# A fused Fourier-mixing and SwiGLU kernel: all units split, value banks seeded from ScalarE, transforms moved to output banks

## The chip, the cores and the metric

The kernel runs on one core of a Trainium2 chip. The metric is the device time of one launch in microseconds. Before the change the median of three runs was 651.96 us (651.83 to 652.64).

## The reference

The input is mixed by the real part of a two-dimensional Fourier transform and then goes, row by row, through a gated feed-forward block:

```python
X = np.fft.fft(np.fft.fft(x, axis=1), axis=2).real      # x: 8 x 3008 x 256
g = X @ w_gate                                          # 24064 x 256 @ 256 x 1536
out = (g / (1 + np.exp(-g)) * (X @ w_val)) @ w_out      # 24064 x 1536 @ 1536 x 256
```

## The kernel before

Half of the sequence rows follow from the other half, because the transform of real data is symmetric. The kernel keeps two factors for each column of a tile (Pt and Qt, up to 512 columns). A *bank* is one buffer of the accumulation memory that matmuls write, 512 float32 columns wide; the kernel allots three to gates (g), three to values (v) and two to outputs (o). A gate or value of the "plus" row is Wp·P + Wq·Q, and that of its mirror, the "minus" row, is Wp·P − Wq·Q, except for a row d = 0 of the weights that enters both with the same sign. A *unit* is one block of 128 of the 1536 hidden columns in one tile: 12 units a tile, 24 tiles.

In an unsplit unit TensorE writes the plus value and then adds Wm·Q (Wm is −2 Wq with the d = 0 row zeroed) to get the minus value: six matmuls with the gate's three. In a *split* unit VectorE takes the half sum `es` out of the v bank before Wq·Q is added, and later forms the minus value as 2·es − v. That saves a matmul and costs VectorE an operation. `bc` is the d = 0 row of Q, broadcast to all partitions. `sv` is one of two buffers that collect the minus values and their SiLUs of a pair of units, which GpSimd multiplies into `hm`; `hp` is VectorE's product for the plus rows. The extracts here and below are shortened: index ranges are left out, and `...` marks other cuts.

```python
psG = tile_pool("psG", bufs=3, PSUM)   # g banks
psV = tile_pool("psV", bufs=3, PSUM)   # v banks
psO = tile_pool("psO", bufs=2, PSUM)   # output banks
...
SPLIT = (0, 1, 2, 3, 5, 6, 7, 8, 9, 11)                  # of 12 units, tiles 3 to 20
SPLIT_END = (0, 1, 2, 3, 4, 6, 7, 8, 9, 10, 11)          # tiles 21 to 23

def part_a(u):                         # TensorE: g, g, v (and v again where unsplit)
    ...
    if split(u):
        v = psV.tile(...)
        mm(v, Wp, 1, Pt, True, False)
        nc.scalar.activation(sg, g, AF.Silu)
        nc.vector.scalar_tensor_tensor(es, bc[t], w0[:, f], v, op0=mult, op1=add)
    ...
def part_b(u):                         # one unit later
    nc.tensor.matmul(g, Wm[:, 0, fs], Qt, start=False)
    if kept:                           # split
        nc.tensor.matmul(v, Wq[:, 1, fs], Qt, start=False)
        vm, sm = sv[:, 0, second], sv[:, 1, second]      # sv: [P, 2, 2, T]
        nc.vector.scalar_tensor_tensor(vm[:, ::-1], es, 2.0, v, op0=mult, op1=subtract)
        nc.scalar.activation(sm[:, ::-1], g, AF.Silu)
        # every second unit: GpSimd multiplies the pair into hm
        nc.vector.tensor_tensor(hp, sp, v, op=mult)
```

Between these parts each unit gives TensorE eight output matmuls of the tile before. A pair of output blocks fills a bank in 24 of them, so ScalarE copies a bank out (`ev`) in units 3, 6, 9 and 0. Fourteen *transform jobs* after the start-up (the first 50 us) produce Pt and Qt for later tiles, each in two halves; both halves were issued after one unit, in two v banks and two g banks, with `od` the copy of the first factor out of its bank. Seven of the jobs also have *one-row matmuls*, which write a single row.

## Time and profile before

| | before |
|---|---|
| median time | 651.96 us |
| span of the profiled run | 650.1 us |
| TensorE, VectorE, ScalarE, GpSimd busy | 98%, 88%, 67%, 72% |
| matmuls | 4218 |
| start-to-start gaps of TensorE, first 50 us / later | 12.2 / 8.7 us |

The last row is worked out from the starts of all matmuls: what lies between two starts beyond the first one's columns at 2.36 columns per ns, gaps of over 30 ns.

In the lines of profiles PE is TensorE, PEld its weight loads, DVE VectorE, ACT ScalarE and POOL GpSimd; L with a number is a line of the kernel. The *chain that ended last* is followed back from the last instruction, at each step to what released it.

This line of the busy time by stretches (columns: stretch, its length, then busy us and count for TensorE, its weight loads, VectorE, ScalarE and GpSimd, then clock and DMA) shows how near VectorE and GpSimd are in the middle:

```profile
200.00:300.00 100.00, 99.39 (x659) 63.17 (x658) 91.97 (x165) 67.03 (x117) 85.73 (x72) 1.00 0.41 107
```

### The profile page before, as it was taken

The numbers are of one execution on the slowest core, as the hardware profiler recorded it, in microseconds if no ns is written. First come the engines' busy times: TensorE is split into PE (matmuls) and PEld (weight loads), VectorE is DVE, ScalarE is ACT, GpSimd is POOL, SyncE is SP. The second block draws the span as 40 slices with busy tenths as digits, with TensorE's granted clock in tenths as the row PEclk, the third lists the DMA queues.
The fourth block names the chain that finished last, engine by engine and source line by source line (L and its number), as shares of the span: only waits on it lengthen the run. The fifth ranks groups of instructions, "written<-read, shape, count | busy, mean of one in ns | idle before, by whom it ended". The sixth has DMA issues, their size and how long they took to land.

```text
span 650.1 us, 12636 instructions
## 1 busy us (share of the span) xinstructions
PE 636.6 (98%) x4218; PEld 407.6 (63%) x4218; DVE 570.1 (88%) x1010; ACT 433.6 (67%) x765; POOL 467.7 (72%) x419
## 2 busy tenths in 40 slices
PE   7989999999999999999999999999999999999997
PEld 5446666666666666666666666666666666666676
DVE  8797668999998999999999989999999899899982
ACT  8576666677667676676676666766766767667663
POOL 8895955798777798897877787878787435544552
PEclk9999999999999999999999999999999999999999
DMA  9657346345215313434134112225111111111112
GB/s 225 125 75 136 107 111 167 96 135 131 76 36 110 102 44 114 125 102 109 40 107 106 48 33 67 59 75 128 50 45 37 42 42 38 45 37 46 49 50 75
DMA packets 46684, 54.36 MB, mean 84 GB/s; under 512 B 6514, under 2 KB 33690, under 8 KB 46618
## 3 DMA queue, kind: packets, MB, share of 16 engines
q1 hardware_dynamic: 43434, 51.19, 29.2%
q0 software_dynamic: 3184, 2.36, 2.6%
q8 instruction: 33, 0.54, 0.3%
q14 instruction: 33, 0.27, 0.2%
HBM read 29.39 MB, written 24.65 MB: 83 GB/s over the span
## 4 chain that ended last, share of the span: by engine, by line
PE 94%; DVE 3%; POOL 1%; ACT 1%; issue 1%; DVEq 0%; ACTq 0%; POOLq 0%
PE o L696 38%; PE g L737 19%; PE v L737 12%; PE g L767 9%; PE v L770 7%; PE v L787 2%; PE v L587 2%; PE g L587 1%; DVE Pt L600 1%; PE g L905 1%; PE g L438 1%; ACT od L595 1%; PE v L438 1%; PE v L564 1%; DVE hp L758 0%
## 5 line engine op out<-in xcount | busy, mean ns | idle before, releaser
L782 POOL TENSOR_TENSOR hm<-sv 128x1024 bf16<-128x1024 f32 (+5 forms) x126 | 249.7, 1986 | 148.1 <-DVE sv L777 138.6
L747 ACT ACTIVATE sp<-g 128x512 f32<-128x512 f32 (+2 forms) x213 | 125.4, 589 | 82.2 <-PE g L737 76.3
L696 PE MATMUL o<-Wo,hp 128*128 128x256 bf16 (+2 forms) x1140 | 169.8, 273 | 0.0
L696 PE MATMUL o<-Wo,hm 128*128 128x256 bf16 (+2 forms) x1140 | 169.7, 273 | 0.0
L749 DVE SCALAR_TENSOR_TENSOR es<-bc,w,v 128x512 f32<-128x512 bf16 (+2 forms) x213 | 155.8, 731 | 5.3 <-PE v L737 5.3
L779 ACT ACTIVATE sv<-g 128x512 f32<-128x512 f32 (+2 forms) x213 | 125.7, 590 | 45.2 <-PE g L767 44.6
L777 DVE SCALAR_TENSOR_TENSOR sv<-es,v 128x512 f32<-128x512 f32 (+2 forms) x213 | 143.9, 676 | 13.3 <-PE v L770 5.1
L696 PEld LDWEIGHTS <-hp 128*128 128x128 bf16 (+2 forms) x1140 | 112.0, 98 | 69.5
L696 PEld LDWEIGHTS <-hm 128*128 128x128 bf16 (+2 forms) x1140 | 111.9, 98 | 69.3 <-issue 0.2
L785 DVE TENSOR_TENSOR hp<-sp,v 128x512 bf16<-128x512 f32 (+2 forms) x213 | 142.6, 669 | 0.0
L737 PE MATMUL g<-Pt,Wp 128*128 128x512 bf16 (+2 forms) x288 | 108.0, 375 | 0.6
L737 PE MATMUL g<-Qt,Wq 128*128 128x512 bf16 (+2 forms) x288 | 108.0, 375 | 0.5 <-DVE Qt L600 0.5
L737 PE MATMUL v<-Pt,Wp 128*128 128x512 bf16 (+2 forms) x288 | 108.0, 375 | 0.0
L767 PE MATMUL g<-Qt,Wm 128*128 128x512 bf16 (+2 forms) x288 | 108.0, 375 | 0.0
L737 PEld LDWEIGHTS <-Wp 128*128 128x128 bf16 x576 | 56.3, 98 | 39.8 <-issue 2.5
L770 PE MATMUL v<-Qt,Wq 128*128 128x512 bf16 (+2 forms) x213 | 79.8, 375 | 0.0
L790 DVE TENSOR_TENSOR hm<-sg,v 128x512 bf16<-128x512 f32 (+2 forms) x75 | 50.8, 678 | 24.6 <-ACT sg L789 17.0
L758 DVE TENSOR_TENSOR hp<-sg,v 128x512 bf16<-128x512 f32 (+2 forms) x75 | 50.8, 678 | 14.4 <-ACT sg L757 11.3
L702 ACT COPY ev<-o 128x512 f32<-128x512 f32 x90 | 52.7, 585 | 9.8 <-PE o L696 6.1
L757 ACT ACTIVATE sg<-g 128x512 f32<-128x512 f32 (+2 forms) x75 | 44.3, 591 | 21.1 <-PE g L737 19.8
L789 ACT ACTIVATE sg<-g 128x512 f32<-128x512 f32 (+2 forms) x75 | 44.4, 593 | 17.7 <-PE g L767 17.5
L737 PEld LDWEIGHTS <-Wq 128*128 128x128 bf16 x363 | 35.5, 98 | 17.4 <-issue 2.9
(168 smaller groups left out, 595.6 us busy)
## 6 DMA issues: line engine op xcount, KB each, us to landing
out_dram<-ev SPq DMA_DIRECT2D x96, 128.0 KB
XA<-in_x_dram SPq DMA_DIRECT2D x32, 256.0 KB
XA<-in_x_dram SPq DMA_DIRECT2D x112, 64.0 KB
XC<-in_x_dram SPq DMA_DIRECT2D x32, 120.0 KB
XC<-in_x_dram SPq DMA_DIRECT2D x105, 32.0 KB
St<-Fc SPq DMA_DIRECT2D x14, 128.5 KB
out_dram<-ev SPq DMA_DIRECT2D x12, 120.0 KB
out_dram<-ev SPq DMA_DIRECT2D x10, 112.0 KB
```

Source lines behind the costliest of these rows:

```text
L696: nc.tensor.matmul(ps[:n, j, :], hts[minus][:, f, c:c + n], Wo[:, f, :], start=(f == 0), stop=(f == nF - 1))
L702: nc.scalar.copy(ev[:, 0:len(pair), :], ps[:, 0:len(pair), :])
L737: nc.tensor.matmul(ps[:, :w], Wt[:, gv, fs], src[:, :w], start=start, stop=stop, skip_group_check=True)
L747: nc.scalar.activation(sg[:, :w], g[:, :w], AF.Silu)
L749: nc.vector.scalar_tensor_tensor(es[:, :w], bc[t][:, :w], w0[:, f:f + 1], v[:, :w], op0=Alu.mult, op1=Alu.add)
L758: nc.vector.tensor_tensor(hts[t][0][:, f, :w], sg[:, :w], v[:, :w], op=Alu.mult)
L767: nc.tensor.matmul(g[:, :w], Wm[:, 0, fs], Qt[:, :w], start=False, stop=True, skip_group_check=True)
L770: nc.tensor.matmul(v[:, :wp], Wq[:, 1, fs], Qt[:, :wp], start=False, stop=True, skip_group_check=True)
L777: nc.vector.scalar_tensor_tensor(vm[:, w - 1::-1], es[:, :w], 2.0, v[:, :w], op0=Alu.mult, op1=Alu.subtract)
L779: nc.scalar.activation(sm[:, w - 1::-1], g[:, :w], AF.Silu)
L782: nc.gpsimd.tensor_tensor(hts[t][1][:, f - n + 1:f + 1, :w], sv[:, 1, 0:n, :w], sv[:, 0, 0:n, :w], op=Alu.mult)
L785: nc.vector.tensor_tensor(hts[t][0][:, f, :wp], sp[:, :wp], v[:, :wp], op=Alu.mult)
```

## The change

The intent: split all units from the fourth tile on to save TensorE 39 matmuls; pay for VectorE's extra work by giving five `es` a tile to ScalarE, which writes bc·w0 into the v bank ahead of the matmul (a *seed*) and copies the bank out after it; let the transforms use an output bank and run by halves, one unit apart. The operands of GpSimd's product are also interleaved in memory.

```diff
-        for q, pool, nm in ((0, psV, "v"), (1, psG, "g")):      # transform
+        for q, pool, nm in ((0, psO, "o"), (1, psG, "g")):
...
-    SPLIT = (0, 1, 2, 3, 5, 6, 7, 8, 9, 11)
-    SPLIT_END = (0, 1, 2, 3, 4, 6, 7, 8, 9, 10, 11)
+    SEEDED = (3, 5, 7, 9, 11)
+    SEEDED_END = (3, 5, 7, 9, 11)
     def split(u):
-        return 3 <= u[0] and u[1] in (SPLIT if u[0] < t_end else SPLIT_END)
+        return u[0] >= 3
+    def seed(u):
+        seeds[u] = psV.tile([P, T], F32, name="v")
+        nc.scalar.activation(seeds[u][:, :w], bc[t][:, :w], AF.Copy, scale=w0[:, f:f + 1])
...
-            mm(v, Wp, 1, Pt, True, False)
+            mm(v, Wp, 1, Pt, not ahead, False)
+            if ahead:
+                nc.scalar.copy(es[:, :w], v[:, :w])
+            else:
                 nc.vector.scalar_tensor_tensor(es, bc[t], w0[:, f:f + 1], v, ...)
...
-            nc.tensor.matmul(v, Wq[:, 1, fs], Qt, ...)
+            nc.tensor.matmul(v, (Wm if seeded(u) else Wq)[:, 1, fs], Qt, ...)
...
-                pending.append(svp.tile([P, 2, 2, T], F32, name="sv"))
+                pending.append(svp.tile([P, 2, T, 2], F32, name="sv"))
...
         part_a(u)
         if owork:
             owork.run(4)
+        if i + 1 < len(units) and seeded(units[i + 1]):
+            seed(units[i + 1])
...
-            whole_part(*job_at[i])
+            transform(*job_at[i])          # one half; the other after the next unit
```

Once, `Wm[:, 1]` is multiplied by −0.5, which makes it Wq without the d = 0 row.

## The prediction

> **What bounds the kernel now.** I began with the page's first part. TensorE is busy for 98% of the span, VectorE for 88%, GpSimd for 72%, ScalarE for 67%.
>
> ```profile
> PE 636.6 (98%) x4218; PEld 407.6 (63%) x4218; DVE 570.1 (88%) x1010; ACT 433.6 (67%) x765; POOL 467.7 (72%) x419
> ```
>
> The 98% alone proves little, since matmuls overlap, so I read starts in the timeline. These lines are one whole unit (one block of 128 hidden columns) in the middle of the kernel; the columns are start us, us, engine, line, operation.
>
> ```profile
> 404.84 0.38 PE L737 MATMUL g<-Pt,Wp 128*128 128x512 bf16 x1
> ...
> 405.05 0.38 PE L737 MATMUL g<-Qt,Wq 128*128 128x512 bf16 x1
> ...
> 405.27 0.38 PE L737 MATMUL v<-Pt,Wp 128*128 128x512 bf16 x1
> ...
> 405.49 0.60 PE L696 MATMUL o<-Wo,hm 128*128 128x256 bf16 x4
> ...
> 405.92 0.38 PE L767 MATMUL g<-Qt,Wm 128*128 128x512 bf16 x1
> ...
> 406.79 0.38 PE L737 MATMUL g<-Pt,Wp 128*128 128x512 bf16 x1
> ```
>
> A 512-column matmul is shown as 0.38 us but the next starts 0.216 us later; four 256-column ones take 0.43. A split unit is five of the first and eight of the second, 5 x 0.216 + 8 x 0.109 = 1.95 us, and it does take 406.79 - 404.84 = 1.95. So TensorE runs end to end here. I summed, over all starts of the trace, what each gap has beyond the matmul's own columns (at 2.36 columns per ns, the rate of these lines): 623 us of columns and 21 us of gaps. 12.2 us of the gaps lie in the first 50 us. The other 8.7 us are nearly all in the 14 transform jobs, as in this piece of the chain that ended last:
>
> ```profile
> 372.32 0.34 PE v L587 x3
> 372.66 0.02 issue
> 372.68 0.48 ACT od L595
> 373.17 0.04 issue
> 373.21 0.49 PE v L587 x3
> ```
>
> The second half of a job waits for the copy out of the first half's v bank. Seven jobs of this kind lose 0.40 us each, seven of the other kind 0.44 in two waits (for a v bank and a g bank): 5.9 us. The remaining 2.6 us are around one-row matmuls and stay.
>
> VectorE, though, is next in line. By groups with shapes apart (busy us, mean ns at the end of each line):
>
> ```profile
> L749 DVE SCALAR_TENSOR_TENSOR es<-bc,w,v 128x512 f32<-128x512 bf16 x192 | 142.6, 743 | 5.1 <-PE v L737 5.1
> L785 DVE TENSOR_TENSOR hp<-sp,v 128x512 bf16<-128x512 f32 x192 | 130.7, 681 | 0.0
> ...
> L790 DVE TENSOR_TENSOR hm<-sg,v 128x512 bf16<-128x512 f32 x60 | 41.3, 688 | 23.2 <-ACT sg L789 16.7 <-PE o L696 6.3
> ...
> L451 ACT CAST Wq<-o 128x512 bf16<-128x512 f32 x5 | 3.0, 593 | 2.2 <-PE o L447 2.2
> ...
> L453 ACT ACTIVATE Wm<-o,m 128x512 bf16<-128x512 f32 x2 | 1.4, 692 | 0.0
> ```
>
> A split unit takes three VectorE operations (0.743, 0.688, 0.681; started back to back 0.67, 0.60 and 0.60 apart, so 1.87 us against TensorE's 1.95), an unsplit one two (0.688 each). That is why not every unit was split: it saves TensorE a matmul and costs VectorE an operation.
>
> **What the Trainium skill says.** (1) "Perfetto Trace Analysis", section Identifying the Most-Contended Engine, says that matmul busy share is a poor measure, as matmuls are pipelined. The trace agrees: 0.38 us shown, 0.216 from start to start. (2) "ScalarE: Activation LUTs", section What ACT_TABLE_LOAD costs, gives about 93 ns more for each per-partition pointer operand and about 93 ns of overlap between back-to-back activations. The trace agrees: with a pointer scale 692 ns (L453) against 593 without (L451), and after a 0.585 us bank copy the next operation starts 0.48 us later. (3) "PSUM — Partial Sum Buffer", section The four PSUM rules: ScalarE's writes leave the has-written bits alone, and a matmul that opens a group clears them over its whole bank. So a seed is added to only where an earlier matmul set the bit, and a 377-column transform in a v bank would leave the later columns to be overwritten. I take this as the reason that transforms leave the v banks; no run here shows it yet. (4) "GPSIMD Engine Reference", section Performance pitfalls for Q7 kernels, puts a slow case at SBUF reads with steps above 8 bytes. The new layout steps by exactly 8, so I expect no loss; the trace of before has only unit steps here and cannot tell.
>
> **The change, part by part.**
>
> *Every unit split from the fourth tile on.* Before, 18 tiles have ten split units and three have eleven; 39 more become split. Each loses one matmul. Two units lie in a 480-column tile and one has 328, so 19720 columns go, 38.5 full matmuls x 0.217 = **8.4 us off TensorE**. That engine sets the end nearly everywhere after 50 us, so this should all reach the end unless something new waits. The instruction order confirms 39 matmuls and 39 weight loads fewer. VectorE pays 39 x (0.743 + 0.688 + 0.681 - 2 x 0.688) = 29 us more. On GpSimd, 39 single products (1.28 us) become parts of pairs (2.36 us): 39 x 1.09 = 42 us more, 468 to 510, 80%.
>
> *Seeds.* 105 units (5 in each of 21 tiles) drop the es operation on VectorE: 105 x 0.743 = 78 us less. With the 29 added, VectorE goes from 570 to 521 us. ScalarE gains a seed (a copy with pointer scale, about 0.59 + 0.10 = 0.70 us, an estimate from the two lines) and a bank copy (0.585): 105 x 1.285 = 135 us, 434 to 569, 89% by busy time. Started back to back each costs 0.1 less, so a tile of 39 operations plus transform copies holds about 20.4 us of ScalarE work in 23.6 us of TensorE work: below the bound, without much room.
>
> *What a seed can hold up.* The seed of unit u must wait for VectorE's last read of the v bank of u-3, and the matmul of u must wait for the seed. Counting from the end of the second v matmul of u-3: VectorE starts 0.2 later (as now) and finishes its two operations at about 1.55; ScalarE has done the SiLU of u-1 by then, so the seed runs from 1.62 to 2.35; TensorE reaches the seeded matmul at 0.43 + 0.65 + 0.43 + 0.43 + 0.43 + 0.43 = 2.80. So 0.45 us of slack. Only where an output copy (ev) comes just ahead of the seed does this fail: output pairs end in units 3, 6, 9 and 0, and of the seeds only that of unit 7 follows in the same slot. There the copy starts at 1.71, the seed at 2.2, and it ends at 2.9 and is seen a little later, 0.15 late. 21 tiles x 0.15 = **3 us given back**.
>
> *Transforms.* Halves one unit apart, the first factor in an output bank, which ScalarE frees within a unit. The wait for the od copy and for the v bank goes; the g bank is freed by VectorE's sums, about 1.6 us after the half, and the next half wants it 2.4 us after. I expect **5.9 us off**. An output bank is free then: pairs switch in units 3 and 6, halves come in 4 and 5.
>
> *One-off.* One scaling of a weight matrix, off the path.
>
> Sum: 652.0 - 8.4 - 5.9 + 3.0 = 640.7; I add 0.3 for unforeseen small waits: **641 us**.
>
> **Rivals.** *ScalarE becomes the next bound.* Chain: VectorE read, seed, matmul, bank copy, matmul. If ScalarE runs later than I count and every seed is late by 0.15, 105 x 0.15 = 16 us come back: 637.7 + 16 = 654, nothing gained. For it: 89% busy and strict order on one queue. Against it: today it idles mostly waiting for TensorE, as the 82.2 us ahead of its first SiLU show, and slack is 0.45 us in most slots. *GpSimd becomes the bound.* In 60 to 500 us it is busy 345 of 440 us; about 18 tiles x 2.2 us more (6 x 2.36 against 4 x 2.36 + 2 x 1.28) makes 385 of 430, 90%, and the stretch 250 to 300 us, with 43.4 of 50 now, comes near full. A pair late by more than two buffers stops VectorE and then TensorE: some 3 to 8 us, 644 to 649. If the 8-byte step also made each product half as long again, GpSimd would need about 28 us per tile and the kernel would pass 700; I hold that unlikely. If interleaving helps the two reads share lines, this rival vanishes. *Everything fits.* No late seeds: 637.7. *Transforms don't gain.* If each half finds a new wait of 0.2 us, the result is about 646.
>
> **Range and chances.** The bottom is the case where everything fits with a little gained in the start-up: 636.5. The top is GpSimd's crowding or transforms that gain nothing: 646.5. A gain of over 2% needs below about 639, more than 13 us of the 14.3 that I can find; that wants almost no late seeds: 0.25. Slower by 2% needs GpSimd's bad case: 0.03. Within 2%: 0.72.
>
> **What will show it right or wrong.** TensorE at 4179 matmuls, still 98% busy; VectorE near 521 us, ScalarE near 569, GpSimd near 510; the seed near 700 ns; the chain of waits without od between transform halves; waits of v matmuls for seeds only around unit 7, some 3 us in all. I am wrong if v matmuls wait for seeds in most units, if VectorE waits for GpSimd's products at the sv buffers, if the product of 1024 elements differs much from 2364 ns, or if the strided writes lengthen the operations that make them (0.688 on VectorE, 0.600 on ScalarE).

## The result and the profile after

The changed kernel took 645.65 us (median of 4 runs, 644.48 to 645.75), the kernel before 652.3 us in the same rounds. Ratios here are the mean time of one kernel's fast runs over that of the other's of the same rounds, so not quite the ratio of the medians: 0.9892, with a 95% interval of 0.9875 to 0.9909. The kernel is faster by 1.1%, which is within the 2% called the same.

The first part of the page of the changed kernel:

```profile
PE 632.8 (98%) x4179; PEld 405.0 (63%) x4179; DVE 522.0 (81%) x945; ACT 532.6 (83%) x975; POOL 452.3 (70%) x419
```

VectorE fell to the 521 us predicted and the 39 matmuls are gone. GpSimd went down, not up. The groups with shapes apart say why, and what the seed costs:

```profile
L794 POOL TENSOR_TENSOR hm<-sv 128x1024 bf16<-128x1024 f32 x114 | 215.9, 1894 | 130.9 <-ACT sv L791 117.1 <-DVE sv L789 12.9
L791 ACT ACTIVATE sv<-g 128x512 f32<-128x512 f32 x228 | 149.7, 656 | 6.3 <-PE g L779 6.3
...
L732 ACT ACTIVATE v<-bc,w 128x512 f32<-128x512 bf16 x95 | 67.1, 707 | 0.5 <-DVE hp L797 0.5
```

The product of a pair takes 1894 ns instead of 2364, ScalarE's SiLU that writes its operand 656 instead of 600, and the seed 707.

Next, a transform half in the chain that ended last (start us, us, what), where before stood an `od` step of 0.48 us:

```profile
371.57 0.33 PE o L587 x3
371.89 0.42 PE o L564 x3
372.31 0.43 PE g L587 x3
372.74 0.42 PE g L564 x3
373.16 0.54 PE g L743 x2
```

TensorE goes from matmul to matmul; no other engine is left in the job. What remains are the 0.09 us steps around the one-row matmuls (L564).

Two new gaps are in the timeline. The first is the one predicted, in unit 7:

```profile
398.36 0.59 ACT L698 COPY ev<-o 128x512 f32<-128x512 f32 x1
...
398.84 0.70 ACT L732 ACTIVATE v<-bc,w 128x512 f32<-128x512 bf16 x1
...
399.24 0.38 PE L743 MATMUL g<-Qt,Wq 128*128 128x512 bf16 x1
...
399.59 0.38 PE L743 MATMUL v<-Pt,Wp 128*128 128x512 bf16 x1
```

The v matmul should start 0.216 us after the g matmul, at 399.46. The seed stands behind the output copy, ends at 399.54, and the matmul starts at 399.59. The second is at a tile's start:

```profile
408.15 0.58 ACT L759 COPY es<-v 128x512 f32<-128x512 f32 x1
...
408.61 0.66 ACT L791 ACTIVATE sv<-g 128x512 f32<-128x512 f32 x1
...
408.91 0.38 PE L919 MATMUL g<-Qt,sel 128*128 128x512 bf16 x1
...
409.32 0.38 PE L743 MATMUL g<-Pt,Wp 128*128 128x512 bf16 x1
```

The broadcast matmul (L919) takes one of the three g banks. The next g matmul needs the bank that the SiLU at 408.61 reads, which ends at 409.27; TensorE waits 0.20 us. The SiLU is late because the copy of unit 11's seeded v bank, at 408.15, is ahead of it.

Where the time went, from the starts of all matmuls in the two traces:

| | us |
|---|---|
| columns saved: 19720 / 2.36 per ns | −8.4 |
| waits in transform jobs | −5.9 |
| gap ahead of unit 7's v matmul, 21 x 0.141 | +3.0 |
| gap at the tile start, 20 x 0.200, less 0.16 there before | +3.9 |
| one more gap at 51 us | +0.2 |
| first 50 us (12.23 to 13.26) | +1.0 |
| sum | −6.2 |

The spans differ by 650.1 − 643.8 = 6.3 us. The start-up's 1.0 us has two parts. Between 40 and 50 us the gaps fall from 1.1 to 0.5 us: one more transform job runs there. Between 10 and 20 us they rise from 3.0 to 4.6, and there the changed kernel's trace has a granted clock of 0.51 from 12.8 to 16.2 us, against 1.00 before. The mean clock differs between executions of one kernel too: the changed kernel's run at a mean clock of 0.999 took 644.48 us, its three at 0.997 took 645.62 to 645.75. Profiled kernels below with a clock of 1.00 in the first 50 us have 11.9 to 13.0 us of gaps there, those with 0.97 have 13.2 to 13.4. The clock need not be all of it: the 13.0 are those of the transforms alone, which lose 1.4 us against the kernel before between 10 and 30 us, at a clock of 1.00. So a difference of about 1 us between medians below says little by itself, and the argument goes by the gaps.

### The profile page after: what moved, and what is told of

It is laid out like the page before. It is cut to its first block, busy times and chain, and to the rows that moved or that the text cites. A ratio compares the mean times of both kernels' runs of the same rounds, so it can differ in the third digit from the quotient of the medians.

```text
span 643.8 us, 12739 instructions
## 1 busy us (share of the span) xinstructions
PE 632.8 (98%) x4179; PEld 405.0 (63%) x4179; DVE 522.0 (81%) x945; ACT 532.6 (83%) x975; POOL 452.3 (70%) x419
## 3 DMA queue, kind: packets, MB, share of 16 engines
q0 software_dynamic: 3184, 2.36, 2.8%
## 4 chain that ended last, share of the span: by engine, by line
PE 95%; DVE 2%; POOL 1%; ACT 1%; issue 1%; DVEq 0%; ACTq 0%; POOLq 0%
PE o L692 38%; PE g L743 19%; PE v L743 11%; PE g L779 9%; PE v L782 8%; PE g L587 2%; PE o L587 2%; PE v L799 1%; PE v L438 1%; PE g L438 1%; PE g L919 1%; DVE hp L770 1%; PE g L564 1%; PE o L447 0%; PE o L564 0%
## 5 line engine op out<-in xcount | busy, mean ns | idle before, releaser
L794 POOL TENSOR_TENSOR hm<-sv 128x1024 bf16<-128x1024 f32 (+2 forms) x126 | 234.1, 1858 | 154.1 <-ACT sv L791 133.9
L789 DVE SCALAR_TENSOR_TENSOR sv<-es,v 128x512 f32<-128x512 f32 (+2 forms) x252 | 170.8, 678 | 73.5 <-PE v L782 69.8
L797 DVE TENSOR_TENSOR hp<-sp,v 128x512 bf16<-128x512 f32 (+2 forms) x252 | 168.9, 670 | 0.0
L791 ACT ACTIVATE sv<-g 128x512 f32<-128x512 f32 (+2 forms) x252 | 162.8, 646 | 6.9 <-PE g L779 6.9
L761 DVE SCALAR_TENSOR_TENSOR es<-bc,w,v 128x512 f32<-128x512 bf16 (+2 forms) x147 | 107.5, 731 | 4.2 <-PE v L743 4.2
L732 ACT ACTIVATE v<-bc,w 128x512 f32<-128x512 bf16 (+2 forms) x105 | 73.2, 697 | 0.5 <-DVE hp L797 0.5
L759 ACT COPY es<-v 128x512 f32<-128x512 f32 (+2 forms) x105 | 60.3, 574 | 0.0
L782 PE MATMUL v<-Qt,Wq 128*128 128x512 bf16 (+2 forms) x147 | 55.1, 375 | 0.0
L157 POOL TENSOR_TENSOR SDf<-XA 128x1020 f32<-128x1020 f32 x14 | 33.0, 2355 | 11.3 <-DMA St<-Fc 6.6
L782 PE MATMUL v<-Qt,Wm 128*128 128x512 bf16 (+2 forms) x105 | 39.4, 375 | 0.0
```

What stands on the lines that cost most here:

```text
L732: nc.scalar.activation(seeds[u][:, :w], bc[t][:, :w], AF.Copy, scale=w0[:, f:f + 1])
L759: nc.scalar.copy(es[:, :w], v[:, :w])
L761: nc.vector.scalar_tensor_tensor(es[:, :w], bc[t][:, :w], w0[:, f:f + 1], v[:, :w], op0=Alu.mult, op1=Alu.add)
L782: nc.tensor.matmul(v[:, :wp], (Wm if seeded(u) else Wq)[:, 1, fs], Qt[:, :wp], start=False, stop=True, skip_group_check=True)
L789: nc.vector.scalar_tensor_tensor(vm[:, w - 1::-1], es[:, :w], 2.0, v[:, :w], op0=Alu.mult, op1=Alu.subtract)
L791: nc.scalar.activation(sm[:, w - 1::-1], g[:, :w], AF.Silu)
```

## The experiments

The theory after the result: the 14.3 us of the matmuls and transforms arrive in full, and seeds give back about half by their place in ScalarE's queue. The main rival: VectorE, or GpSimd, would be the bound without seeds and interleaving, so that what they cost is a price worth paying. Twelve kernels were run, each with 5 rounds, each set of four on one chip. All outputs are right. In four traces (split alone, no seeds, old layout, seeds 3-5-8) some 67 to 69 matmul records are missing; a place where exactly one matmul is missing is not counted as a gap.

| kernel | median us | ratio to before |
|---|---|---|
| changed, first / again | 645.65 / 645.58 | 0.9892 / 0.9885 |
| transforms alone | 646.34 | 0.9903 |
| split alone | 646.65 | 0.9898 |
| both, no seeds, old layout | 639.58 | 0.9797 |
| changed without seeds | 640.27 | 0.9804 |
| changed, old layout | 643.42 | 0.9858 |
| changed, no seed in unit 11 | 642.20 | 0.9843 |
| changed, seed ahead of output copy | 642.75 | 0.9844 |
| both of these | 639.71 | 0.9806 |
| changed, seeds 3, 5, 8 | 640.27 | 0.9803 |
| changed, seeds 4, 7, 10 | 649.25 | 0.9941 |
| both parts, broadcast in an output bank | 638.06 | 0.9775 |

**Transforms alone**, on the kernel before:

```diff
-        for q, pool, nm in ((0, psV, "v"), (1, psG, "g")):
+        for q, pool, nm in ((0, psO, "o"), (1, psG, "g")):
...
+        for eo in range(2):                   # the halves in two successive units
```

> The kernel before with only the transform part of the change: halves one unit apart, first factor in an output bank. Theory (the 5.9 us of waits in the transform jobs go, whatever the rest does): 646 us against 652, ratio 0.991; gaps above 0.12 us at the transforms gone after 50 us, only the one-row matmuls' 0.09 us gaps left. Rival (these waits go only because VectorE is less loaded in the full change): VectorE at 88% makes the sums late, new waits at g banks appear and no more than 2 us is gained, 650 us or more.

646.34 us, ratio 0.9903. The later gaps fell from 8.7 to 3.0 us, 2.6 of them around one-row matmuls. The theory holds, although VectorE was still at 88%.

**Split alone**, on the kernel before:

```diff
-    SPLIT = (0, 1, 2, 3, 5, 6, 7, 8, 9, 11)
-    SPLIT_END = (0, 1, 2, 3, 4, 6, 7, 8, 9, 10, 11)
+    SPLIT = tuple(range(12))
+    SPLIT_END = tuple(range(12))
```

> The kernel before with only the split of all units from the fourth tile on, no seeds, transforms and layout as before. Theory (VectorE would become the bound): a tile asks VectorE for 12 x 1.87 us plus about 1.5 us of sums, 23.9 us, against 23.6 of TensorE, so the 8.4 us saved come back in part: 646 to 652 us, VectorE near 96% busy in the middle, TensorE waiting at v banks for VectorE. Rival (the seeds are not needed, TensorE sets the end all the same): 643.6 us with no new waits.

646.65 us, ratio 0.9898. The time is at the edge of what the theory allowed, but for another reason. Of the 8.4 us, 6.7 arrived ((1 − 0.9898) x 652). The gaps of the old transform jobs stay (2.9 us of od waits, 1.0 between the other halves, 3.1 ahead of the next g matmul, which includes the one-row steps), 0.5 us more in all than before, and those at the tile start are 1.2 us instead of 0.16. In the middle, where VectorE is 96% busy, no unit's v matmul waits for it. It is waited for five times, in the old transform jobs (L587) and just after them (columns: us in total, times, longest):

```profile
PE v L587 <- DVE hp L785: 0.9, 3, 0.3
...
PE g L737 <- DVE Pt L600: 0.7, 2, 0.5
```

The expectation's count was wrong: it set VectorE's 23.9 us a tile against 23.6 of TensorE without TensorE's own share of the transforms. Those are 7 jobs of about 2.3 us and 7 of 1.9, so 1.4 us per tile: TensorE needs some 25 us a tile, VectorE 23.9.

**Changed without seeds:**

```diff
-    SEEDED = (3, 5, 7, 9, 11)
-    SEEDED_END = (3, 5, 7, 9, 11)
+    SEEDED = ()
+    SEEDED_END = ()
```

> The changed kernel without seeds: every es on VectorE. Theory (seeds pay because VectorE would be the bound): VectorE about 599 us busy, 93% overall and some 96% in the middle; the two seed gaps (0.13 us in unit 7, 0.20 us at the tile start) gone, 6.9 us, but VectorE's backlog after the transform sums gives back 3 to 10 us: 641 to 649. Rival (seeds are pure loss): 638.7 us, no gaps but the one-row matmuls' ones.

640.27 us, ratio 0.9804: close to the rival of "pure loss" (638.7). The same stretch as shown for the kernel before:

```profile
200.00:300.00 100.00, 99.31 (x655) 63.97 (x666) 97.39 (x176) 71.17 (x120) 85.03 (x74) 1.00 0.39 106
```

VectorE is 97% busy and TensorE does not wait for it: after 50 us there are the one-row steps and 20 gaps at the tile start, mostly 0.09 us (mean 0.11; one, at 329 us, is 0.36), nothing else. So the seeds were not needed.

**Changed, old layout:**

```diff
-                pending.append(svp.tile([P, 2, T, 2], F32, name="sv"))
+                pending.append(svp.tile([P, 2, 2, T], F32, name="sv"))
-            vm, sm = sv[:, int(second), :, 0], sv[:, int(second), :, 1]
+            vm, sm = sv[:, 0, int(second)], sv[:, 1, int(second)]
...                                       # and the product's operands
```

> The changed kernel with the product's operands in separate rows as before, not interleaved. Theory (interleaving makes GpSimd's product faster and ScalarE's SiLU write slower): product back from 1894 to about 2364 ns, GpSimd from 452 to about 510 us, SiLU write back from 656 to 600 ns; the tile-start gap shrinks from 0.20 to about 0.14 us, so about 1 us faster than the changed kernel if GpSimd's load does no harm, 644.5. Rival (GpSimd at 90% in the middle crowds the sv buffers): VectorE waits for the product, TensorE in turn, 3 to 8 us slower, 648 to 653.

643.42 us, ratio 0.9858, faster than with interleaving. GpSimd rose to 509 us. The gap at the tile start fell from 0.200 to 0.151 us in 20 tiles, 1.0 us; the unit-7 gap stayed at 0.142. VectorE's waits for GpSimd add up to some 6 us and none reaches TensorE. Of the rest of the 2.2 us, 0.8 is in the start-up (12.5 against 13.3 us); what is left was not traced further. The gaps alone carry the reading that interleaving costs about 1 us.

**Both parts alone** (split and transforms on the kernel before; neither seeds nor interleaving):

```diff
+    SPLIT = tuple(range(12))
+    SPLIT_END = tuple(range(12))
...
+        for q, pool, nm in ((0, psO, "o"), (1, psG, "g")):
...
+            job_at[u] = (b, part, (eo,))
```

> The kernel before with all units split from the fourth tile on and the transforms by halves through output banks; no seeds, no interleaving. Theory (these two parts are the whole gain and seeds and interleaving only cost): tile-start gap 0.06 us as with the split alone, instead of 0.11 with the interleaved layout, so about 1 us below the kernel without seeds: 639.0 us, ratio 0.979, GpSimd 510 us busy. Rival (GpSimd near full without interleaving crowds the sv buffers once TensorE is faster): VectorE waits for the product and the ratio is 0.982 or more.

639.58 us, ratio 0.9797. The two parts multiply: 0.9898 x 0.9903 = 0.9802. The tile-start gap is 0.04 us in most tiles; two, of 0.15 and 0.32 us, lift the mean to about 0.06 and were not traced to a cause. The groups, for comparison with the interleaved ones above:

```profile
L782 POOL TENSOR_TENSOR hm<-sv 128x1024 bf16<-128x1024 f32 x114 | 269.9, 2367 | 76.2 <-DVE sv L777 75.9
...
L779 ACT ACTIVATE sv<-g 128x512 f32<-128x512 f32 x228 | 136.6, 599 | 44.1 <-PE g L767 42.1 <-PE v L770 1.6 <-POOL BBa L180 0.3
```

Against the kernel without seeds (0.9804, interleaved) the ratios do not differ beyond their intervals; in the gaps the interleaving shows as 0.05 us per tile, 0.09 against 0.04 in most.

**No seed in unit 11:**

```diff
-    SEEDED = (3, 5, 7, 9, 11)
+    SEEDED = (3, 5, 7, 9)            # and SEEDED_END
```

> The changed kernel with four seeds a tile (3, 5, 7, 9), none in unit 11. Theory (the new 0.20 us gap ahead of the first g matmul of each tile comes from unit 11's bank copy on ScalarE, which stands ahead of the SiLU that frees the g bank): the gap vanishes in 20 tiles, 4.0 us off, 641.6 us, ratio 0.983. Rival (the gap comes from the strided, 56 ns longer SiLU write or from the broadcast matmul's extra g bank itself): the gap stays at 0.15 to 0.2 us and the time stays near 645.5.

642.20 us, ratio 0.9843. The tile-start gap fell from 0.200 to 0.094 us, 2.1 us in 20 tiles, not to zero. So unit 11's copy is half of it, and the rival's other sources are the rest. Medians over the 20 tiles, which leave odd tiles out, give the parts: 0.198 with seeds and interleaving, 0.148 with seeds alone, 0.089 with interleaving alone (0.090 here) and 0.039 with neither. Seeds cost 0.11 and interleaving 0.05 whichever way it is taken, and the 0.04 are there without both.

**The seed ahead of the output copy:**

```diff
         part_a(u)
+        if i + 1 < len(units) and seeded(units[i + 1]):
+            seed(units[i + 1])
         if owork:
             owork.run(4)
-        if i + 1 < len(units) and seeded(units[i + 1]):
-            seed(units[i + 1])
```

> The changed kernel with the seed emitted ahead of the output copy on ScalarE. Theory (only a seed that stands behind an output copy is late): the 0.13 us gap ahead of the v matmul of unit 7 goes in 21 tiles, 2.8 us off, 642.9 us, ratio 0.985; the gap at the tile start stays. Rival (ScalarE is short of time in that slot whatever the order): the wait moves to another operation, such as the SiLU that frees a g bank, and the time stays within 1 us of 645.6.

642.75 us, ratio 0.9844. ScalarE's timeline in unit 6:

```profile
396.18 0.60 ACT L756 ACTIVATE sp<-g 128x512 f32<-128x512 f32 x1 [0.27 <-PE g L743]
396.70 0.69 ACT L732 ACTIVATE v<-bc,w 128x512 f32<-128x512 bf16 x1
397.33 0.58 ACT L698 COPY ev<-o 128x512 f32<-128x512 f32 x1
```

The seed goes first and all 21 gaps of 0.141 us are gone; the 20 at the tile start stay at 0.200.

**Both edits together:**

```diff
+    SEEDED = (3, 5, 7, 9)            # and the seed ahead of owork.run(4)
```

> Both of the previous two edits together: seeds at 3, 5, 7, 9 and each ahead of the output copy. Theory: the two gaps are independent and add, 6.8 us off, 638.8 us, ratio 0.979. Rival (removing one gap lets another appear, because ScalarE or VectorE is close to the bound): less than 5 us off, above 640.6.

639.71 us, ratio 0.9806. Later gaps fell from 9.9 to 4.5 us; the two effects add (3.0 + 2.1), and no other gap appears. The time is 0.9 us above the 638.8 expected; the expectation took the tile-start gap for gone, and 1.9 us of it remain.

**Three seeds, placed well and badly:**

```diff
+    SEEDED = (3, 5, 8)               # none behind an output copy
```

> The changed kernel with three seeds a tile, in units 3, 5 and 8: none follows an output copy and none is in unit 11. Theory (place of the seeds, not their number, makes the gaps): both gaps gone, 6.9 us off, 638.7 us, ratio 0.979, with perhaps 1 us given back by VectorE (two more es a tile, 521 to 552 us busy). Rival (VectorE's backlog after the transform sums makes the seed of unit 8 late): gaps of 0.1 to 0.5 us ahead of the v matmul of unit 8 in the 14 tiles with transforms, 640.5 or more.

```diff
+    SEEDED = (4, 7, 10)              # each behind an output copy
```

> The changed kernel with three seeds a tile as in the kernel with seeds at 3, 5 and 8 (ratio 0.9803), but at 4, 7 and 10, each behind an output copy. Theory (a seed behind an output copy is late by 0.13 to 0.14 us): 3 x 21 x 0.135 = 8.5 us slower than that kernel, about 648.5 us, ratio 0.993, with gaps ahead of the v matmuls of units 4, 7 and 10. Rival (the number of seeds or ScalarE's load counts, not their place): the same time as seeds at 3, 5 and 8, ratio 0.980.

640.27 and 649.25 us, ratios 0.9803 and 0.9941 (intervals 0.9788 to 0.9817 and 0.9927 to 0.9954), at equal VectorE (549 and 550 us) and ScalarE load (499 us both). In the chain of the second, three units apart, the v matmul's step is 0.34 us, and 0.22 between:

```profile
401.53 0.34 PE v L743
...
403.61 0.22 PE v L743
...
405.56 0.22 PE v L743
...
407.51 0.34 PE v L743
```

There are 63 such gaps of 0.140 us, 8.8 us. With seeds at 3, 5 and 8 there is none, so the rival of a late unit 8 fell; the 638.7 us expected there were missed because the tile-start gap stays, at 0.09 us as in every kernel without a seed in unit 11 but with interleaving. Place in the queue decides, not the number of seeds.

**The broadcast in an output bank**, on the kernel with both parts alone:

```diff
         if f == 0 and split((t, SPLIT[0])):
-            ps = psG.tile([P, T], F32, name="g")
+            ps = psO.tile([P, T], F32, name="o")
```

> The previous kernel with the broadcast matmul of each tile's start in an output bank instead of a g bank. Theory (the tile-start gap is the wait for a g bank, because the broadcast takes one of three): the gap of 0.06 us in some 19 tiles goes, 1.2 us off, ratio 0.977. Rival (the broadcast in an output bank waits for the output copy, or makes the next output group wait): a new gap of 0.1 us or more ahead of the broadcast or of an output matmul, ratio as the previous kernel or worse.

638.06 us, ratio 0.9775 (0.9763 to 0.9787), the fastest kernel and the only one whose gain is over 2% with its whole interval. The tile-start gap is gone, and 2.7 us of later gaps remain, all but 0.1 around one-row matmuls. In the middle:

```profile
200.00:300.00 100.00, 100.00 (x671) 64.35 (x669) 97.47 (x177) 68.86 (x121) 95.55 (x75) 1.00 0.39 105
```

VectorE is at 97%, GpSimd at 96% and TensorE never stops. The interval overlaps that of the kernel with both parts alone (0.9784 to 0.981), so the gain of this last edit rests on the gaps, not on the times.

**The changed kernel again**, as an anchor in these rounds:

> The changed kernel once more, unedited, so that it shares the rounds of the three above: ratio 0.989, 645.5 us.

645.58 us, ratio 0.9885 (0.987 to 0.99).

## Why the prediction was right or wrong

The time, 645.65 us, lies in the range, near its top, and "within 2%" held. In part that is luck: the top of the range stood for GpSimd's crowding or for transforms that gain nothing, neither of which came, and a loss that the prediction did not have took their place. Two of the signs that it named for being wrong did show: the product at 1894 ns instead of 2364, and ScalarE's strided write at 656 ns instead of 600 (VectorE's stayed at 689 against 688). Step by step:

*Matmuls saved, 8.4 us.* Right: 39 fewer, and with the split and transform parts alone 13 us of the 14.3 arrive.

*Transforms, 5.9 us.* Right in mechanism and size: shown by the transforms alone.

*Seeds, 3 us given back in unit 7.* Right: 21 gaps of 0.141 us (0.15 predicted), made to vanish by reordering and tripled by moving all seeds behind output copies. The rival that every seed is late (654 us) fell.

*What was missing.* The sum failed by 4.7 us, and most of it is one term that it lacked: "what a seed can hold up" followed only the chain of the v bank. Its copy also delays the SiLU behind it, which frees a g bank, and at a tile's start the broadcast takes one of the three. That is the 0.200 us in 20 tiles: 0.11 from unit 11's copy, 0.05 from the longer SiLU write, and a rest of 0.04 that goes when the broadcast leaves the g banks. So of the 6.9 us of new gaps after 50 us, seeds made 5.1 and interleaving 1.0. The other 1.0 us were in the start-up: 1.6 us lost where the clock dipped, less 0.6 gained by the transform job there.

*GpSimd, 510 us.* Wrong: 452. The step that failed is the 2.36 us taken for a pair's product in the new layout ("I expect no loss"); it became 20% faster, 1894 ns. Without interleaving it is 509 us, as worked out. The rival that GpSimd would crowd the sv buffers fell in both layouts.

*ScalarE, 569 us.* Sized wrong: 533. The added operations took 73.2 + 60.3 = 133.5 us (135 predicted), but adding them to a busy time forgets that back-to-back records overlap by about 0.1 us and count once: 170 ScalarE records overlapped the next before, 598 after.

*Why not every unit was split before.* Here the prediction gave a reason that the runs refute. VectorE's 1.87 us against 1.95 was read as leaving no room. With all 12 units on VectorE and the transforms in output banks it is 97% busy and holds nothing up, since TensorE also has the transforms to do; with the old transforms TensorE waits for it five times, 1.6 us in all, and 6.7 of the 8.4 us still arrive. The prediction named "everything fits" as the best case and did not ask whether the seeds were needed at all; without them the kernel is 0.9% faster (0.9804 against 0.9892), half of what the change could have brought.

## What to carry to other kernels

Before work is moved off an engine that looks nearly full, run the version that leaves it there: an engine at 97% that is never waited for costs nothing. When an operation is put on a queue with strict order, follow not only what it produces but every operation that it pushes back, and ask which bank or buffer each of those frees. Judge a saturated TensorE by the starts of its matmuls: each record overlaps the next by 0.16 us here, which hides the gap of 0.141 us wholly and that of 0.200 us nearly.

## What the Trainium skill lacked or had wrong

- "GPSIMD Engine Reference", section Performance pitfalls for Q7 kernels: it names a cost above 8 bytes of step, but not that two operands interleaved word by word, at a step of exactly 8 bytes, can be read faster than two separate rows: 1893 to 1895 ns for a product of 1024 elements against 2364 to 2368. Why is not shown.
- "SBUF — State Buffer", section Specifications (TRN2): two accesses per 16-byte line are said to be enough for full bandwidth, which a step of 8 bytes gives. ScalarE's backward write at that step took 647 to 659 ns instead of 599 to 606 at a step of 4; VectorE's backward write did not change (687 to 689 against 685 to 688).
- "PSUM — Partial Sum Buffer", section Summary: rules for kernel authors, says that a seed written by ScalarE must be zero. Seeds other than zero gave the right result in all seven seeded kernels run here, where earlier matmuls of the same or a greater width had written the bank; that is what the same page's section The four PSUM rules lets one expect. No run put a transform in a seeded bank, so the reason to keep them apart stays the page's.
